# Strassen's seven products for three more chunks of a fused Fourier mixing and gated convolution kernel

## The chip, the cores and the metric

The kernel runs on one core of a Trainium2 chip. Its time is the device time of one launch in microseconds; it is given as the median of several runs. The profile is of one execution of the program on the chip, with the time of every instruction on each engine: PE (matrix products), PEld (the loading of a product's stationary operand, which runs beside PE), DVE (vector work), ACT (activations and copies), POOL (GpSimd) and SP (a queue that issues transfers). All values are 32-bit floating point. PE does a product of 32-bit values in two passes, so that one matmul of the program is two instructions of the profile.

## The reference

```
X = np.fft.fft(x, axis=1); X = np.fft.fft(X, axis=2); x = X.real     # x: 8 x 3136 x 256
h = np.maximum(x @ w_in, 0.0)                                        # w_in: 256 x 1024
conv_out = conv_w[0]*h[s-1] + conv_w[1]*h[s] + conv_w[2]*h[s+1]      # along the sequence
gate = 1 / (1 + exp(-conv_out))
return (h * gate) @ w_out                                            # w_out: 1024 x 256
```

## The kernel before

**Stages of a batch.** There are 8 batches b = 0 to 7 (the text calls b = 3 the fourth). The real Fourier transform along the sequence uses its symmetries: x of a batch is *folded* on DVE (sums and differences of rows and columns, `fold_ops`, 16 pieces per batch, L155 to L193 and L228), then eight *units* (`units`) multiply the folded x by tables of sines and cosines on PE (tiles `pd<-tab,w`) and put the results together on DVE (`fin`, L369 to L431, *unit sums*) into two tiles `pt` and `qt`. A unit has a PSUM bank `pd`, of which there is one; so a unit's first matmul waits until the DVE has read the sums of the unit before it.

**Chunks and steps.** A batch's outputs are made in 4 chunks c of rows; chunks 0, 1 and 2 have six tiles of 128 rows, chunk 3 six and a rest. Each chunk goes over 8 blocks f of 128 hidden features. A *step* is one (b, c, f): 32 steps per batch, 256 in all, numbered 32b + 8c + f. For a step, PE makes two products with `pt` and `qt` (`pb`, `pa`), ACT copies `pb` (L841), DVE combines the two to h with the ReLU (L849, twice), ACT makes the first tap (L855), a transfer of POOL's queue adds the middle one (L859), DVE the last (L864); ACT takes the sigmoid (L883), DVE the gate's product (L891), and then PE multiplies the gated rows by a block of w_out into `po` banks (`mm2`, L94), summed over the chunk's eight f. There are four `po` banks, given out in turn; each holds two row tiles of 256 columns. After f = 7 ACT copies the banks out (L1000) and SP writes them.

**What sets the order.** One loop over t writes every engine's queue by hand. In its round t stand: the sigmoid of step t-4, the products of step t+1 and their copies, the combine of t, the first tap of t, the last tap of t-3, the gate of t-4, the transfer of t, and the second product (`mm2`) of step t-5 (`LAG` is 5). Everything else (folds, units, loads, weights) is put beside it by `at(cycle, where, fn)`: in round `cycle`, at one of the places "first", "act", "dve", "late", "pool", "load" and "pe" of the round. `ends[b]` is the round by which the folds of batch b end and its units begin; the folds spread from `ends[b-1]` to `ends[b]`, one per round at most, and `free` finds a round not yet in `taken`; the units spread from `ends[b]` to the round 32b - 3. "late" (unit sums) is behind the gate on DVE, "dve" (folds, w_out's sums) between the combine and the last tap, "pe" behind `mm2`.

**Strassen's products.** `seven(s)` says for which chunks row tiles 4 and 5 are multiplied by Strassen's method in Winograd's form: for two f at a time, the 2 by 2 blocks of rows and features (`a11` to `a22`, 128 x 128 each) take seven matmuls of 128 columns in place of four of 256. Before, these are the chunks of the last two batches, but for the very last. In an odd f (round t with step t-5 odd), DVE makes four sums of the gated rows (`sums`, L933 to L936, tile `sv`); three of the seven products stand in `mm7` of that round, and the other four, which read `sv`, at the head of `mm2` of the next (`rest`). Differences of w_out's blocks (`forms`, L920, tile `TW`, four pieces) are made once. At the chunk's end the two banks `x` and `y` of the seven products are put together by one ACT copy (L967) and four DVE additions (`end`, L971 to L974), which stand behind everything of DVE's next round, since `rest` comes first. Such a chunk takes four `po` banks: two for row tiles 0 to 3, and `x` and `y`.

Of the kernel before, what the change touches and what calls it, by code (L numbers as in the profile page):

```python
# [37 lines left out]
def kernel(  # L38
# [11 lines left out]
    B, S, D = x.shape  # L50
# [11 lines left out]
    NF = F // P  # L62
# [30 lines left out]
    def mm(o, l, r, start, stop):  # L93
        nc.tensor.matmul(o, l, r, start=start, stop=stop, skip_group_check=True)  # L94
# [13 lines left out]
    def load_ops(b, h, eng, other=None, held=False):  # L108


        def plain():
            t = xp.tile([P, 8, 2, D], F32, name="xh", tag="xh")
            xh[b, h] = t
            if held:

                nc.gpsimd.memset(t[0:1, 0, 0, 0:1], 0.0)
            eng.dma_start(out=t[0:NP, 0:4], in_=bass.AP(
                tensor=x.tensor, offset=x.offset + (b * S + 1 + 2 * h) * D,
                ap=[[HQ * D, NP], [Q4 * D, 4], [1, 2 * D]]))

        def zero():
            t = xh[b, h]
            for s0, n, r in ((0, 4, 0), (4, 3, 1), (7, 1, 0)):
                (other or eng).dma_start(out=t[NP:KR, s0:s0 + n], in_=bass.AP(
                    tensor=x.tensor, offset=x.offset + (b * S + r * Q4) * D,
                    ap=[[D, 1], [Q4 * D, n], [0, 2], [1, D]]))

        def mirrored(m):
            def f():
                nc.gpsimd.indirect_dma_start(  # L130
                    out=xh[b, h][0:NP, 7 - m].rearrange("p q d -> p (q d)"),
                    out_offset=None,
                    in_=bass.AP(tensor=x.tensor, offset=x.offset,
                                ap=[[2 * D, B * S // 2], [1, 2 * D]]),
                    in_offset=bass.IndirectOffsetOnAxis(ap=idx[0:NP, 0:1], axis=0),
                    element_offset=(b * S + (4 - m) * Q4 - HO + 2 * (1 - h)) * D)
            return f
        return [plain] + [zero] * h + [mirrored(m) for m in range(4)]
# [451 lines left out]
    def spread(b, cs):  # L590

        for c in cs:
            ch = chunks[c]
            eb[b, c] = ebp.tile([P, HN], F32, name="eb", tag="eb")[:, 0:ch.k1 - ch.k0]
            nc.sync.dma_start(out=eb[b, c], in_=ed[b:b + 1, ch.k0:ch.k1].to_broadcast([P, ch.k1 - ch.k0]))
# [31 lines left out]
    chunks = [Chunk(c) for c in range(len(CUTS))]  # L627
# [132 lines left out]
    begin, us, row, flip, store, odd_first, even_first = units(0)  # L760
# [141 lines left out]
            nc.scalar.copy(out=left[:, f, b % 2 * LEFT:(b % 2 + 1) * LEFT], in_=gs[s][:, r])  # L902

    TW = {}
    due, ends_of = [], []

    def seven(s):

        b, c, f = s
        return b >= B - 2 and not (chunks[c].last and b % 2)  # L910

    def forms(i):

        one, two = wout[:, 0:NF:2], wout[:, 1:NF:2]
        b11, b12, b21, b22 = one[:, :, 0:P], one[:, :, P:D], two[:, :, 0:P], two[:, :, P:D]
        if i == 0:
            t = erp.tile([P, 4, NF // 2, P], F32, name="tw", tag="er")
            TW.update({k: t[:, j] for j, k in enumerate((5, 7, 6, 4))})
        k, x, y = ((5, b12, b11), (7, b12, b22), (6, b11, TW[7]), (4, b21, TW[6]))[i]
        vt(TW[k], x, y, op=ALU.subtract)  # L920

# [21 lines left out]
    def mm7(s):  # L943
# [9 lines left out]
        mm(x[:, 1], a12, wout[:, f, 0:P], False, last)  # L953
        mm(y[:, 0], a22, TW[4][:, m], m == 0, last)

        def rest():
            t = sums_of.pop(s)
            mm(y[:, 1], t[:, 0], TW[5][:, m], False, last)
            mm(y[:, 2], t[:, 1], TW[7][:, m], False, last)
            mm(x[:, 2], t[:, 2], TW[6][:, m], False, last)  # L960
# [17 lines left out]
    def mm2(s):  # L978
# [10 lines left out]
        if seven(s):  # L989
            tiles = tiles[:4]  # L990
# [15 lines left out]
        if not seven(s):  # L1006
            gs.pop(s)
        elif f % 2:
            mm7(s)
            gs.pop(s)  # L1010
            gs.pop((b, c, f - 1))
# [14 lines left out]
    ops, _, pres = fold_ops(0)  # L1026
# [43 lines left out]
    n = chunks[0].k1  # L1070
# [16 lines left out]
    per = len(chunks) * NF  # L1087
    LAG = 5
# [3 lines left out]
    taken = set()  # L1092

    def at(cycle, where, fn):
        side.setdefault((cycle, where), []).append(fn)
# [20 lines left out]


    ends = [9, 25, per + 13, 2 * per + 6][0:B] + [per * (b - 1) - 3 + max(11 - 4 * (b - 2), 0) for b in range(4, B)]
    def free(cycle):

        while cycle in taken:
            cycle += 1
        taken.add(cycle)
        return cycle

    for i in range(4):
        at(per * (B - 2) + i, "dve", lambda i=i: forms(i))
    feat = Feature()
    at(5, "load", feat.place)
    at(8, "dve", feat.signs)  # L1130
# [10 lines left out]
    for b in range(1, B):  # L1141
        begin, us, *_ = units(b)
        us = us[0:2] + us[5:7] + us[2:4] + us[7:] if b == 1 else us[0:4] + us[5:]

        c0 = ends[b] - 3 * (b == 1)
        n = per * b - (2 if b == 1 else 3) - c0
        at(max(c0, per * (b - 1) + 1), "pe", begin)
        cs = [c0 + i * n // len(us) for i in range(len(us) + 1)]
        if b > 1:
            cs[1:] = [c + (-1 if i == len(us) else 1) * (c % NF == LAG % NF) for i, c in enumerate(cs[1:], 1)]  # L1150
        for i, u in enumerate(us):
            k = cs[i + 1] - cs[i]
            j0 = int(b == B - 1)
            for j in range(j0, k):
                at(cs[i] + j, "pe", lambda u=u, j=j - j0, k=k - j0: u.matmuls(j, k))
            at(cs[i + 1], "act", u.copy)
            at(cs[i + 1], "late" if b > 1 else "dve", u.fin)
            if b > 1:
                taken.add(cs[i + 1])
        at(cs[-1] - 2, "load", lambda b=b: spread(b, range(len(chunks) - 2)))  # L1160
        at(per * b + 1, "load", lambda b=b: spread(b, [len(chunks) - 2]))
        at(per * b + NF, "load", lambda b=b: spread(b, [len(chunks) - 1]))
    for b in range(1, B):
        ops, singles, pres = fold_ops(b)
        c0, n = ends[b - 1], ends[b] - ends[b - 1]
        if b == 1:

            cs = [9, 11, 12, 13, 14, 16, *range(16, 26)]
            assert len(cs) == len(ops) and cs[-1] <= ends[1] and not taken & set(cs)
        else:  # L1170
            if b == 2:
                c0, n = c0 + 3, n - 3
            cs = [free(c0 + j * n // len(ops)) for j in range(len(ops))]
            assert cs[-1] < ends[b]
        if b + 1 < B:
            for h in range(2):
                for j, fn in enumerate(load_ops(b + 1, h, nc.sync)):
                    at(cs[len(ops) // 2 * (h + 1) - 1] + 1 + j, "load", fn)
        for j, fn in enumerate(ops):
            at(cs[j], "dve", fn)  # L1180
        for j, fn in singles.items():
            at(cs[j], "pool", fn)
        for j, fn in pres.items():
            at(cs[j], "act", fn)
# [3 lines left out]
    n = len(steps)  # L1188
# [6 lines left out]
    for t in range(n + LAG):  # L1195
# [20 lines left out]
        if t >= LAG and seven(steps[t - LAG]) and steps[t - LAG][2] % 2:  # L1216
            run_later = sums(steps[t - LAG])
        else:
            run_later = None
# [82 lines left out]
```

## Time and profile before

| | |
|---|---|
| median of 3 runs | 1147.53 us (1147.52 to 1147.59) |
| the profiled execution | 1147.18 us, its span 1145.4 us |
| busy on PE, DVE, ACT, POOL | 1127.9, 997.5, 892.1, 387.3 us |
| granted clock of PE | 1.0 |

The span is from the first to the last instruction, and what the time has beyond it (1.8 us) lies around it. A matmul's duration in the profile reaches until its results have drained, and the next one starts before that; so a row of n passes is best read by the distance from its start to the start of the next row. In a timeline a row is: start, length, engine, line, operation, out<-in, tile, count, and in brackets the idle time before it and who ended it.

### The profile page before, as it was taken

To read this page: it belongs to the slowest core of one execution; us is meant where nothing else is said; L and a number is where in the kernel's file an instruction comes from. 1 tells how busy PE (TensorE), PEld (TensorE's weight loads), DVE (VectorE), ACT (ScalarE), POOL (GpSimd) and SP (SyncE) were. 2 spreads that over 40 slices of the span, in tenths; PEclk is the share of its full clock that TensorE was granted. 3 is DMA by queue.
4 is the path that set the end of the run, shared out by engine and by line. 5 is a ranking of instruction groups with operands and counts; after the bars stand their busy time and mean duration, and the time that the engine had idled before them with its cause. 6 is when DMAs were issued, how large, how long until landed. Compare 5 with 4: busy or idle time off the path is not lost.

```text
span 1145.4 us, 15566 instructions
## 1 busy us (share of the span) xinstructions
PE 1127.9 (98%) x4992; PEld 889.4 (78%) x4992; DVE 997.5 (87%) x1596; ACT 892.1 (78%) x1700; POOL 387.3 (34%) x486
## 2 busy tenths in 40 slices
PE   6999999999999999999999999999999999999998
PEld 4777877788777877877777777777777888778777
DVE  8999899988888989888878888888887888898885
ACT  3788778877787778787878877887876878888884
POOL 5426523543345252424233232422222222222223
PEclk9999999999999999999999999999999999999999
DMA  8787985876767686757676766766655656666663
GB/s 238 193 131 160 171 169 113 189 168 137 169 129 162 127 194 142 175 117 158 136 174 135 152 136 125 180 139 124 135 118 101 137 119 139 139 142 130 129 123 95
DMA packets 107678, 167.53 MB, mean 146 GB/s; under 512 B 32174, under 2 KB 62920, under 8 KB 107597
## 3 DMA queue, kind: packets, MB, share of 16 engines
q0 software_dynamic: 42240, 115.87, 53.0%
q1 hardware_dynamic: 64616, 50.53, 15.7%
q8 instruction: 40, 0.66, 0.2%
q14 instruction: 41, 0.34, 0.1%
q10 hardware_dynamic: 741, 0.14, 0.1%
HBM read 37.80 MB, written 25.74 MB: 55 GB/s over the span
## 4 chain that ended last, share of the span: by engine, by line
PE 92%; DVE 5%; ACT 1%; issue 1%; POOL 0%; DVEq 0%; ACTq 0%
PE po L94 57%; PE pa L94 14%; PE pb L94 14%; PE pd L94 6%; DVE g L864 1%; DVE h L849 1%; DVE g L891 1%; DVE xh L166 0%; DVE xh L155 0%; DVE wout L662 0%; ACT nb L841 0%; ACT os L1000 0%; ACT g L883 0%; ACT pa L820 0%; DVE w L193 0%
## 5 line engine op out<-in xcount | busy, mean ns | idle before, releaser
L94 PE MATMUL po<-wout,g 128*128 128x256 f32 (+1 forms) x2960 | 669.2, 375 | 1.2 <-DVE g L891 1.1
L94 PEld LDWEIGHTS po<-wout,g 128*128 128x128 f32 x2960 | 553.8, 190 | 129.8 <-issue 16.9
L859 POOL DMA_DIRECT2D g<-h x256 | 219.7, 858 | 710.3 <-ACT g L855 406.5
L841 ACT ACTIVATE nb<-pb 128x386 f32<-128x386 f32 (+3 forms) x512 | 228.3, 501 | 194.5 <-PE pb L94 193.7
L849 DVE CUSTOM_DVE_ANT_0 h<-pa,nb 128x386 f32<-128x386 f32 (+3 forms) x512 | 265.5, 560 | 33.1 <-PE pa L94 14.3
L891 DVE TENSOR_TENSOR g<-g,h 128x770 f32<-128x770 f32 (+1 forms) x248 | 240.9, 971 | 48.6 <-ACT g L883 47.5
L864 DVE SCALAR_TENSOR_TENSOR g<-h,cw,g 128x770 f32<-128x770 f32 (+1 forms) x256 | 265.3, 1036 | 1.5 <-DMA g<-h 1.4
L883 ACT ACTIVATE g<-g,cw 128x770 f32<-128x770 f32 (+3 forms) x264 | 246.8, 938 | 16.3 <-DVE g L864 16.2
L855 ACT ACTIVATE g<-h,cw 128x770 f32<-128x770 f32 (+1 forms) x256 | 244.5, 955 | 0.0
L94 PE MATMUL pb<-qt,G 127*128 127x387 f32 (+2 forms) x512 | 213.5, 498 | 1.5 <-ACT nb L841 1.1
L94 PE MATMUL pa<-pt,G 128*128 128x387 f32 (+2 forms) x512 | 212.2, 495 | 1.0 <-ACT pa L820 0.7
L820 ACT ACTIVATE pa<-eb,ge 128x387 f32<-128x387 f32 (+2 forms) x256 | 155.6, 608 | 1.0 <-DVE h L849 0.4
L94 PEld LDWEIGHTS pa<-pt,G 128*128 128x128 f32 x512 | 96.6, 189 | 75.6 <-issue 19.0
L130 POOL DMA_INDIRECT xh<-in_x_dram,idx x64 | 100.3, 1567 | 19.3 <-issue 10.1
L94 PEld LDWEIGHTS pb<-qt,G 127*128 127x128 f32 x512 | 90.4, 190 | 8.3 <-ACT nb L841 2.7
L94 PE MATMUL pd<-tab,w 98*128 98x197 f32 (+2 forms) x448 | 94.5, 318 | 0.0
L94 PEld LDWEIGHTS pd<-tab,w 98*128 98x128 f32 (+1 forms) x448 | 79.5, 191 | 7.5
L1000 ACT COPY os<-po 128x256 f32<-128x256 f32 x182 | 53.5, 394 | 7.7 <-PE po L94 7.7
L177 POOL COPY w<-xh 98x4 f32<-98x4 f32 (+1 forms) x30 | 45.7, 1523 | 6.7 <-DVE xh L171 6.7
L155 DVE TENSOR_TENSOR xh<-xh 98x1020 f32<-98x1020 f32 (+1 forms) x32 | 38.7, 1213 | 0.7 <-DMA xh<-in_x_dram,idx 0.5
L166 DVE TENSOR_TENSOR xh<-xh 98x1024 f32<-98x1024 f32 (+1 forms) x32 | 38.9, 1216 | 0.1
L94 PEld LDWEIGHTS po<-tw,sv 128*128 128x128 f32 x168 | 23.0, 190 | 8.1 <-issue 2.5
(167 smaller groups left out, 538.0 us busy)
## 6 DMA issues: line engine op xcount, KB each, us to landing
g<-h POOLq DMA_DIRECT2D x192, 385.0 KB, 4.1
g<-h POOLq DMA_DIRECT2D x64, 416.0 KB, 4.3
out_dram<-os SPq DMA_DIRECT2D x96, 256.0 KB
xh<-in_x_dram SPq DMA_DIRECT2D x16, 784.0 KB
eb<-ed SPq DMA_DIRECT2D x16, 193.5 KB
raw<-in_moe_w_in_dram SPq DMA_DIRECT2D x4, 512.0 KB
raw<-in_moe_w_out_dram SPq DMA_DIRECT2D x1, 2048.0 KB
eb<-ed SPq DMA_DIRECT2D x8, 209.0 KB
```

The source lines that it names most:

```text
L94: nc.tensor.matmul(o, l, r, start=start, stop=stop, skip_group_check=True)
L130: nc.gpsimd.indirect_dma_start(out=xh[b, h][0:NP, 7 - m].rearrange("p q d -> p (q d)"), out_offset=None, in_=bass.AP(tensor=x.tensor, offs ...
L177: nc.gpsimd.tensor_copy(w[k, 0:2, qs, 0], t()[k, s:s + 2, :, 0])
L820: act(pa[s][:, 0:n], eb[b, c], AF.Copy, scale=ge[:, f:f + 1])
L841: act(nb[s][:, i, cols], p[:, cols], AF.Copy, scale=-1.0 if i else 1.0)
L849: nc.vector._custom_dve(TENSOR_ADD_SAT, out=to, in0=a[:, cols], in1=c[:, i, cols], s0=BIG, s1=0.0)
L855: act(gs[s], hs[s][:, 0:n], AF.Copy, scale=cw[:, 0, s[2]:s[2] + 1])
L859: nc.gpsimd.dma_start(out=gs[s], in_=hs[s][:, 1:1 + n], accum_op=ALU.add)
L864: stt(out=g, in0=h[:, k:k + n], scalar=cw[:, k, f:f + 1], in1=g, op0=ALU.mult, op1=ALU.add)
L883: act(gs[s][:, c], gs[s][:, c], AF.Sigmoid, scale=cw[:, 1, s[2]:s[2] + 1])
L891: vt(g, g, h[:, 0:r.stop], op=ALU.mult)
L1000: nc.scalar.copy(out=osb[:, j % 2], in_=pt[:, j % 2])
```

## The change

Chunk 1 of batches 3, 4 and 5 joins those multiplied by the seven products (`EXTRA`). The four pieces of w_out's differences move from rounds 192 to 195 to rounds 77, 95, 99 and 103. The rounds of a chunk of `EXTRA` in which DVE makes the four sums or the end (the five per chunk in `summing`: 110, 112, 114, 116 and 117 for batch 3) are closed to folds and to unit sums, which move to other rounds. `ends` of batches 5, 6 and 7 goes from 125, 157 and 189 to 128, 164 and 197, so that these folds end later and the units have 29, 25 and 24 rounds in place of 32; the last round of the units stays. The amount of fold and unit work is the same.

```
+    EXTRA = ((3, 1), (4, 1), (5, 1))
     def seven(s):
         b, c, f = s
-        return b >= B - 2 and not (chunks[c].last and b % 2)
+        return b >= B - 2 and not (chunks[c].last and b % 2) or (b, c) in EXTRA
...
+    ends[B - 3:] = [e + d for e, d in zip(ends[B - 3:], (3, 7, 8))]
...
-    for i in range(4):
-        at(per * (B - 2) + i, "dve", lambda i=i: forms(i))
+    for i, c in enumerate((77, 95, 99, 103)):
+        at(c, "dve", lambda i=i: forms(i))
+    summing = {per * b + NF * c + LAG + i for b, c in EXTRA for i in (1, 3, 5, 7, 8)}
+    taken.update(summing)
...
-            cs[1:] = [c + (-1 if i == len(us) else 1) * (c % NF == LAG % NF) for i, c in enumerate(cs[1:], 1)]
+            for i in range(1, len(cs)):
+                cs[i] += (-1 if i == len(us) else 1) * (cs[i] % NF == LAG % NF)
+                while cs[i] in summing:
+                    cs[i] += -1 if i == len(us) else 1
...
-            cs = [free(c0 + j * n // len(ops)) for j in range(len(ops))]
+            cs = [c for c in range(c0, c0 + n) if c not in taken]
+            if b > 4:
+                cs = [cs[j * len(cs) // len(ops)] for j in range(len(ops))]
+                taken.update(cs)
+            else:
+                cs = [free(c0 + j * n // len(ops)) for j in range(len(ops))]
```

On DVE, in rounds 110 and 111 (chunk 1 of batch 3 is in its second product there), stood before:

```order
L849 ISA h<-pa,nb 128x386 x2
L864 SCALAR_TENSOR_TENSOR g<-h,cw,g 128x770
L891 TENSOR_TENSOR g<-g,h 128x770
L381 TENSOR_TENSOR qt<-as,pd 128x393
L383 TENSOR_TENSOR qt<-pd,as 128x392
L849 ISA h<-pa,nb 128x386 x2
L155 TENSOR_TENSOR xh<-xh 99x4x255
L864 SCALAR_TENSOR_TENSOR g<-h,cw,g 128x770
L891 TENSOR_TENSOR g<-g,h 128x770
```

and in the same rounds now (its lines are one higher than the profile's behind the new line):

```order
L849 ISA h<-pa,nb 128x386 x2
L934 TENSOR_TENSOR sv<-g 128x128
L935 TENSOR_TENSOR sv<-g 128x128
L936 TENSOR_TENSOR sv<-sv,g 128x128
L864 SCALAR_TENSOR_TENSOR g<-h,cw,g 128x770
L937 TENSOR_TENSOR sv<-g,sv 128x128
L891 TENSOR_TENSOR g<-g,h 128x770
L849 ISA h<-pa,nb 128x386 x2
L864 SCALAR_TENSOR_TENSOR g<-h,cw,g 128x770
L891 TENSOR_TENSOR g<-g,h 128x770
L381 TENSOR_TENSOR qt<-as,pd 128x393
L383 TENSOR_TENSOR qt<-pd,as 128x392
```

The unit sums moved from round 110 to 111, the fold from 111 out of the pair (to 108), and the four sums stand alone in round 110.

On DVE at the end of that chunk, rounds 117 and 118, before:

```order
L849 ISA h<-pa,nb 128x386 x2
L166 TENSOR_TENSOR xh<-xh 99x1024
L864 SCALAR_TENSOR_TENSOR g<-h,cw,g 128x770
L891 TENSOR_TENSOR g<-g,h 128x770
L849 ISA h<-pa,nb 128x386 x2
L864 SCALAR_TENSOR_TENSOR g<-h,cw,g 128x770
L891 TENSOR_TENSOR g<-g,h 128x770
L427 TENSOR_TENSOR as<-pd,as 128x196
L428 TENSOR_TENSOR as<-pd,as 128x196
```

and now:

```order
L849 ISA h<-pa,nb 128x386 x2
L864 SCALAR_TENSOR_TENSOR g<-h,cw,g 128x770
L891 TENSOR_TENSOR g<-g,h 128x770
L972 TENSOR_TENSOR os<-os,po 128x256
L973 TENSOR_TENSOR os<-os,po 128x256
L974 TENSOR_TENSOR os<-os,po 128x128
L975 TENSOR_TENSOR os<-os,po 128x256
L849 ISA h<-pa,nb 128x386 x2
L864 SCALAR_TENSOR_TENSOR g<-h,cw,g 128x770
L891 TENSOR_TENSOR g<-g,h 128x770
L427 TENSOR_TENSOR as<-pd,as 128x196
L428 TENSOR_TENSOR as<-pd,as 128x196
```

The fold piece left round 117, the chunk's end came in behind the gate, and the unit sums of round 118 stayed where they were.

On PE at the same place (the products of steps 117 and 118, and behind each the second product and a unit's matmuls), before:

```order
L94 MATMUL pb<-qt,G 128x387
L94 MATMUL pa<-pt,G 128x387
L94 MATMUL po<-wout,g 128x256 x6
L94 MATMUL pd<-tab_112,w 128x197
L94 MATMUL pb<-qt,G 128x387
L94 MATMUL pa<-pt,G 128x387
L94 MATMUL po<-wout,g 128x256 x6
L94 MATMUL pd<-tab_112,w 128x197
```

and now:

```order
L94 MATMUL pb<-qt,G 128x387
L94 MATMUL pa<-pt,G 128x387
L94 MATMUL po<-wout,g 128x256 x4
L94 MATMUL po<-wout,g 128x128 x2
L94 MATMUL po<-tw,g 128x128
L94 MATMUL pd<-tab_112,w 128x197
L94 MATMUL pb<-qt,G 128x387
L94 MATMUL pa<-pt,G 128x387
L94 MATMUL po<-tw,sv 128x128 x3
L94 MATMUL po<-wout,sv 128x128
L94 MATMUL po<-wout,g 128x256 x6
L94 MATMUL pd<-tab_112,w 128x197 x2
```

The last pair of the chunk is split into three products in one round and four in the next, in front of the six ordinary ones with which chunk 2 begins; and a unit matmul more stands in the second round.

More of the change, by code (lines that the diff above doesn't have):

```diff
@@ L1149 @@
         if b > 1:
-            cs[1:] = [c + (-1 if i == len(us) else 1) * (c % NF == LAG % NF) for i, c in enumerate(cs[1:], 1)]
+            for i in range(1, len(cs)):
+                cs[i] += (-1 if i == len(us) else 1) * (cs[i] % NF == LAG % NF)
+                while cs[i] in summing:
+                    cs[i] += -1 if i == len(us) else 1
+            for i in range(len(us) - 1, 0, -1):
+                while cs[i] >= cs[i + 1] or cs[i] in summing:
+                    cs[i] -= 1
         for i, u in enumerate(us):
```

## The prediction

> **What bounds the kernel.** I began with the page: busy times, then the chain that ended last.
>
> ```profile
> span 1145.4 us, 15566 instructions
> PE 1127.9 (98%) x4992; PEld 889.4 (78%) x4992; DVE 997.5 (87%) x1596; ACT 892.1 (78%) x1700; POOL 387.3 (34%) x486
> PE 92%; DVE 5%; ACT 1%; issue 1%; POOL 0%; DVEq 0%; ACTq 0%
> ```
>
> PE is the bound: 98% of the span, 92% of the chain. A busy PE need not be full, so I next took the groups of PE instructions of 200 to 1110 us with the idle time before them (last column):
>
> ```profile
> L94 PE MATMUL po<-wout,g 128*128 128x256 f32 x2363 | 545.0, 379 | 0.0
> L94 PE MATMUL po<-tw,sv 128*128 128x128 f32 x162 | 22.4, 274 | 0.0
> ```
>
> PE waits for nobody there, with Strassen's products or without. So the change gains what its passes save on PE, and loses what new waits of PE cost; shorter work elsewhere gains nothing.
>
> **What the passes save.** The 379 and 274 ns above reach until the results are out, so they are not the price. The price is the distance between starts. First an ordinary round of chunk 0 to 2 without a unit, then two rounds with Strassen's products (timeline of PE):
>
> ```profile
> 803.07 0.81 PE L94 MATMUL pb<-qt,G 127*128 127x387 f32 x2
> 804.37 2.75 PE L94 MATMUL po<-wout,g 128*128 128x256 f32 x12
> 806.96 0.49 PE L94 MATMUL pb<-qt,G 127*128 127x387 f32 x1
> ...
> 1036.19 0.82 PE L94 MATMUL pb<-qt,G 127*128 127x387 f32 x2
> 1037.50 0.83 PE L94 MATMUL po<-tw,sv 128*128 128x128 f32 x6
> 1038.16 0.39 PE L94 MATMUL po<-wout,sv 128*128 128x128 f32 x2
> 1038.39 1.89 PE L94 MATMUL po<-wout,g 128*128 128x256 f32 x8
> 1040.12 0.82 PE L94 MATMUL pb<-qt,G 127*128 127x387 f32 x2
> 1041.42 2.33 PE L94 MATMUL po<-wout,g 128*128 128x256 f32 x12
> 1043.59 0.39 PE L94 MATMUL po<-tw,g 128*128 128x128 f32 x2
> 1043.82 0.49 PE L94 MATMUL pb<-qt,G 127*128 127x387 f32 x1
> ```
>
> A pass of 256 columns takes (806.96 - 804.37) / 12 = 0.2158 us. Of a pair's 14 short passes, eight read `sv`: 1038.39 - 1037.50 = 0.89. The x12 row at 1041.42 holds 8 long passes and 4 short ones, so the four take 2.17 - 8 x 0.2158 = 0.44, and the last two 0.23. Fourteen take 1.56 us; the eight long ones that they replace take 1.73. A pair saves 0.17. The whole rounds say the same within rounding: two ordinary ones 2 x 3.89 = 7.78, the pair 1043.82 - 1036.19 = 7.63, so 0.15. Three chunks have four pairs each: 12 x 0.15 = 1.8 to 12 x 0.17 = 2.0 us. I take 1.95. Unit matmuls only change rounds on PE: nothing.
>
> The Trainium skill (TensorE: Matmul & The Clock Gate, section on loading the stationary operand and on the back-to-back gap) says that a weight load takes its columns over 1.2 GHz, about 107 ns for 128, and that in a real stream the spacing is set by load and matmul together. If loads did not overlap here, my estimate by that page is 14 x 0.107 against 8 x 0.107, 0.64 more per pair against the 0.17 saved, +5.6 us in all. The trace disagrees on the overlap: eight short passes in 0.89 us, 111 ns each, leave no room for it.
>
> **What DVE gets in these rounds.** Durations of the added and the moved work (instructions on `sv`; groups of DVE, 500 to 860 us; w_out's differences):
>
> ```profile
> L936 DVE TENSOR_TENSOR sv<-g,sv x28: 281/285/1225, 896.0 to 1109.6; 128x128 f32<-128x128 f32 x28
> ...
> L166 DVE TENSOR_TENSOR xh<-xh 99x1024 f32<-99x1024 f32 x6 | 7.3, 1216 | 0.0
> L155 DVE TENSOR_TENSOR xh<-xh 99x1020 f32<-99x1020 f32 x6 | 7.3, 1210 | 0.0
> L192 DVE TENSOR_TENSOR w<-xh 99x508 f32<-99x508 f32 x6 | 4.1, 678 | 0.0
> ...
> L920 DVE TENSOR_TENSOR tw<-wout x2: 680/680/681, 865.9 to 870.6; 128x512 f32<-128x512 f32 x2
> ```
>
> And the load of DVE in the eight rounds 110 to 117 before, beside eight of batch 6 that have the seven products already (columns: PE, PEld, DVE, ACT, POOL busy):
>
> ```profile
> 511.26:545.16 33.90, 33.90 (x145) 27.02 (x145) 29.24 (x43) 26.06 (x48) 13.96 (x15) 1.00 0.74 164
> 918.00:952.00 34.00, 34.00 (x173) 27.85 (x172) 29.27 (x58) 26.38 (x47) 7.31 (x9) 1.00 0.58 116
> ```
>
> Rounds 110 to 117 lose two pieces of L155, one of the two of L166 and the pair L192 and L193: 1.21 + 1.21 + 1.22 + 1.36 = 5.0 us. They get 16 sums of 0.285 (4.6) and the end of the chunk, 1.57 (rows below). DVE has 29.24 - 5.0 + 6.1 = 30.3 us of work in 33.9 - 4 x 0.17 = 33.2: 91%, no worse than the 29.27 of 34.0 that batch 6 runs with an unstalled PE. The moved folds land in rounds without such work, at most one a round. Nothing of it reaches PE, since DVE's lag is covered: the four sums of round 110 are read by PE in round 111, behind the products that stand there. If that cover were gone, a late sum would cost PE as much as it is late. The pieces of w_out's differences (0.68 each) come between two folds or unit sums, and the next round takes them up. The loads of x move with the folds, by some rounds on SP and POOL's queue; the halves of batches 6 and 7 are still asked for ten rounds and more (3.9 us or longer each) before they are folded, so I cost them at nothing. On ACT a chunk has one narrow copy in place of two of its six.
>
> One rule of the skill bears on this (SBUF — State Buffer, who interferes with whom): a DVE instruction with two inputs in SBUF and a GpSimd one that reads SBUF block each other. The maximum of 1225 ns on L936 beside its median of 285 agrees in kind: one of 28 was held up. POOL's copies of folded columns could so make single sums 0.9 us later, which the cover of a round takes.
>
> **The chunk's end: two PSUM places.** This is where PE could newly wait. Chunk 2 begins in round 117 and takes three `po` banks at once; its third is the bank `x` of the seven products, which only DVE's third end addition frees. In batches 6 and 7 the next chunk takes `x` a round or more later, but for once. Round 205 of batch 6 has the same products, copies and widths:
>
> ```profile
> 922.14 1.19 ACT L1000 COPY os<-po 128x256 f32<-128x256 f32 x4
> 923.24 0.81 PE L94 MATMUL pb<-qt,G 127*128 127x387 f32 x2
> 923.34 0.99 ACT L883 ACTIVATE g<-g,cw 128x770 f32<-128x770 f32 x1
> 924.36 0.96 DVE L891 TENSOR_TENSOR g<-g,h 128x770 f32<-128x770 f32 x1 [1.61 <-ACT g L883]
> 925.21 0.39 PE L94 MATMUL po<-wout,sv 128*128 128x128 f32 x2
> 925.44 1.89 PE L94 MATMUL po<-wout,g 128*128 128x256 f32 x8
> 925.64 0.42 DVE L971 TENSOR_TENSOR os<-os,po 128x256 f32<-128x256 f32 x1 [0.31 <-PE po L94]
> 926.55 0.29 DVE L973 TENSOR_TENSOR os<-os,po 128x128 f32<-128x128 f32 x1
> 927.17 0.52 PE L94 MATMUL pd<-tab,w 98*128 98x196 f32 x2
> 927.21 1.02 DVE L849 CUSTOM_DVE_ANT_0 h<-pa,nb 128x386 f32<-128x386 f32 x2
> ```
>
> The third addition has read `x` at 926.84, and DVE goes on with the next round at 927.21, so that the end costs it 1.57. The fifth tile's matmul would start after eight long passes, at 927.17. The slack is 0.33 us, though the gate before had waited 1.61 for ACT. The one place where the next chunk does take `x` at once, at 1115.40, bears it out:
>
> ```profile
> 1115.40 2.79 PE L94 MATMUL po<-wout,g 128*128 128x256 f32 x12
> 1118.02 0.59 PE L94 MATMUL po<-wout,left 128*128 128x256 f32 x2
> ```
>
> Twelve passes in 2.62, against 12 x 0.2158 = 2.59: a wait of 0.03. I take 0.0 to 0.1 for the three places together.
>
> The second place is the one bank `pd`. Round 118 has unit sums right behind the end; PE's next unit matmul needs their reads of `pd` (L427, L428) done. Before:
>
> ```profile
> 545.16 0.81 PE L94 MATMUL pb<-qt,G 127*128 127x387 f32 x2
> 547.40 1.02 DVE L849 CUSTOM_DVE_ANT_0 h<-pa,nb 128x386 f32<-128x386 f32 x2
> 550.23 0.96 DVE L891 TENSOR_TENSOR g<-g,h 128x770 f32<-128x770 f32 x1 [0.88 <-ACT g L883]
> 551.66 0.35 DVE L428 TENSOR_TENSOR as<-pd,as 128x196 f32<-128x196 f32 x1
> 553.30 0.36 PE L94 MATMUL pd<-tab,w 99*128 99x99 f32 x2
> ```
>
> DVE began that round 2.24 behind step 118's products (547.40 - 545.16), and the slack was 553.30 - 552.01 = 1.29. In round 206, behind an end, it began 927.21 - 923.24 = 3.97 behind them: 1.73 later. Yet DVE then no longer idles 0.88 before the gate, and PE has between the same two points eight short passes on `sv` (0.89) and a second unit matmul more: 1.29 - 1.73 + 0.88 + 0.89 = 1.33 us of slack without that matmul. Cost nothing; if the 0.88 and the 0.89 were missing, PE would wait 0.44 a place.
>
> **Sum.** -1.95 + 0.05 = -1.9 us on the profiled execution, 1147.18 to 1145.3. The median of the runs shown lies 0.35 above that execution, so 1147.53 - 1.9 = 1145.6. That is 0.17% less, inside the 0.2% (2.3 us) about what a measurement of this kernel can tell from no change.
>
> **Rivals.**
> *The end comes late and PE waits for `x`* (slower). For it: only 0.33 us of slack, three times, and DVE's gate hangs on ACT's copies there. Against: round 117 has no fold and no unit sums, ACT there has no scaling and no unit copy, as in round 205. Each microsecond beyond 0.33 costs one, three times. It decides (above 1149.8) from 1.95 + 2.3 = 4.25 us, 1.4 a place. A DVE that came to round 117 a whole fold and a unit's sums behind (1.2 + 1.1, less the slack of 0.33) would give 3 x 2.0 = 6.0: 1151.6.
> *Half a wait.* `x` or `pd` late by 0.3 to 0.6 each time: 1 to 1.9 us, and the gain is eaten: 1146.6 to 1147.5, within 0.2%.
> *Weight loads set the pace* (the change then does not do what it says). If a load's 0.178 us (889.4 over 4992 on the page) could not overlap, 14 x 0.178 against 8 x 0.2158 is +0.77 a pair: 1147.5 + 9.2 = 1156.7. Against: 28 pairs already run at 111 ns a pass. The skill's rule above is the same mechanism at another price.
> *More is saved than the passes* (faster by over 0.2%). It needs 0.4 us more. PE's idle column is 0.0, so only small stalls at the start of products are to be had.
>
> **How the numbers follow.** Forecast 76%, half a wait 7%, late end or other new wait of PE 9%, weight loads 1%, more saved 7%. So faster 0.07, same 0.83, slower 0.10. The range goes from 1145.2 (2.0 saved and 0.3 more) to 1147.4 (half a wait).
>
> **What would show it.** In the changed profile a pair of chunk 1 in batches 3 to 5 is 0.15 to 0.17 us shorter on PE, less its unit matmuls; the first twelve passes of chunk 2 in round 117 take 2.59 to 2.65; the first `pd` matmul after round 118's unit sums starts without idle time; DVE busy grows by 12 x 1.14 + 3 x 1.57 = 18 us, and the idle column of PE stays 0.0. I am wrong if PE waits for DVE's end or for `sv` in these rounds.

## The result and the profile after

The changed kernel takes 1145.88 us (median of 22 runs, 1145.03 to 1146.94) against 1147.57 for the kernel before in runs between them (also 22): a ratio of 0.9984, 95% interval 0.9978 to 0.999. That is 1.7 us less, where 1.9 was forecast, and within 0.2% of no change. The profiled execution took 1145.46 us against 1147.18. Its page, the same lines as of before:

```profile
span 1143.7 us, 15776 instructions
PE 1127.2 (99%) x5064; PEld 890.4 (78%) x5064; DVE 1011.2 (88%) x1656; ACT 889.9 (78%) x1697; POOL 397.7 (35%) x486
PE 94%; DVE 3%; ACT 1%; issue 1%; DMA 0%; POOL 0%; DVEq 0%; ACTq 0%
```

and the groups of PE instructions of 200 to 1108 us:

```profile
L94 PE MATMUL po<-wout,g 128*128 128x256 f32 x2268 | 524.5, 379 | 0.0
L94 PE MATMUL po<-tw,sv 128*128 128x128 f32 x234 | 32.3, 274 | 0.0
```

PE has 72 instructions more (14 passes in place of 8 in each of 12 pairs), and its idle column is still 0.0. DVE has 13.7 us more work.

The time before about 370 us differs between executions, although nothing changes there but for one w_out difference in e9: the products of step 77 began at 369.97 to 371.23 us in the twelve traces of this study. So I compare one stretch in all of them, from the products of step 77 to those of step 255, the last. It holds every other change. Before (columns: PE, PEld, DVE, ACT, POOL busy, PE's clock, DMA share, GB/s):

```profile
370.06:1118.45 748.39, 748.39 (x3354) 595.10 (x3353) 646.26 (x1051) 600.12 (x1112) 214.46 (x276) 1.00 0.66 139
```

and after:

```profile
370.28:1116.73 746.45, 746.45 (x3426) 595.64 (x3425) 659.52 (x1111) 598.04 (x1109) 223.47 (x276) 1.00 0.66 140
```

748.39 - 746.45 = 1.94 us, on 12 pairs 0.162 each; the sum had 1.95. The start of this execution was 0.22 later, which makes 1.72 of the profiled time.

**The pair.** The first pair of chunk 1 of batch 3 has three of its products in round 110 and four in round 111. PE in these two rounds, before:

```profile
515.51 0.81 PE L94 MATMUL pb<-qt,G 127*128 127x387 f32 x2
...
519.40 0.50 PE L94 MATMUL pd<-tab,w 98*128 98x196 f32 x2
519.73 0.81 PE L94 MATMUL pb<-qt,G 127*128 127x387 f32 x2
...
523.63 0.50 PE L94 MATMUL pd<-tab,w 98*128 98x196 f32 x2
```

and after:

```profile
514.51 0.82 PE L94 MATMUL pb<-qt,G 127*128 127x387 f32 x2
...
518.21 0.52 PE L94 MATMUL pd<-tab,w 98*128 98x196 f32 x2
518.57 0.81 PE L94 MATMUL pb<-qt,G 127*128 127x387 f32 x2
...
519.87 0.83 PE L94 MATMUL po<-tw,sv 128*128 128x128 f32 x6
...
520.76 1.89 PE L94 MATMUL po<-wout,g 128*128 128x256 f32 x8
522.49 0.50 PE L94 MATMUL pd<-tab,w 98*128 98x196 f32 x2
```

From the products to the unit's matmuls the two rounds took 3.89 + 3.90 = 7.79 us and take 3.70 + 3.92 = 7.62: 0.17 less. The eight short passes on `sv` are 520.76 - 519.87 = 0.89, as they were in batch 7.

**The chunk's end.** Rounds 117 and 118, on PE and DVE (timeline):

```profile
545.68 2.76 PE L94 MATMUL po<-wout,g 128*128 128x256 f32 x12
545.88 0.42 DVE L972 TENSOR_TENSOR os<-os,po 128x256 f32<-128x256 f32 x1 [0.26 <-PE po L94]
546.79 0.29 DVE L974 TENSOR_TENSOR os<-os,po 128x128 f32<-128x128 f32 x1
547.45 1.02 DVE L849 CUSTOM_DVE_ANT_0 h<-pa,nb 128x386 f32<-128x386 f32 x2
548.27 0.87 PE L94 MATMUL pd<-tab,w 98*128 98x197 f32 x4
550.96 0.37 DVE L427 TENSOR_TENSOR as<-pd,as 128x196 f32<-128x196 f32 x1 [0.69 <-ACT as L418]
551.24 0.35 DVE L428 TENSOR_TENSOR as<-pd,as 128x196 f32<-128x196 f32 x1
552.87 0.36 PE L94 MATMUL pd<-tab,w 99*128 99x99 f32 x2
```

The twelve passes with which chunk 2 begins take 548.27 - 545.68 = 2.59 us, so its fifth tile did not wait for bank `x`. The third addition was done at 547.08, and that tile stood at 545.68 + 8 x 0.2158 = 547.41: 0.33 later. DVE had 0.26 in hand ahead of the end, for it waited there for PE's last product of the chunk. Round 118's unit sums had read `pd` at 551.59, 1.28 ahead of PE's next unit matmul.

### The profile page after: what moved, and what is told of

Read it like the earlier page. It is cut to its first block, busy times and chain, and to the rows that moved or that the text cites. A ratio compares the mean times of both kernels' runs of the same rounds, so it can differ in the third digit from the quotient of the medians.

```text
span 1143.7 us, 15776 instructions
## 1 busy us (share of the span) xinstructions
PE 1127.2 (99%) x5064; PEld 890.4 (78%) x5064; DVE 1011.2 (88%) x1656; ACT 889.9 (78%) x1697; POOL 397.7 (35%) x486
## 4 chain that ended last, share of the span: by engine, by line
PE 94%; DVE 3%; ACT 1%; issue 1%; DMA 0%; POOL 0%; DVEq 0%; ACTq 0%
PE po L94 58%; PE pb L94 15%; PE pa L94 15%; PE pd L94 6%; DVE g L864 1%; DVE h L849 1%; DVE g L891 1%; DVE wout L662 0%; ACT nb L841 0%; ACT os L1001 0%; DMA raw<-in_moe_conv_w_dram 0%; ACT g L883 0%; ACT pa L820 0%; ACT g L855 0%; DVE raw L668 0%
## 5 line engine op out<-in xcount | busy, mean ns | idle before, releaser
L94 PE MATMUL po<-wout,g 128*128 128x256 f32 (+1 forms) x2912 | 653.9, 373 | 1.2 <-DVE g L891 1.1
L94 PEld LDWEIGHTS po<-wout,g 128*128 128x128 f32 x2912 | 542.0, 190 | 124.6 <-issue 16.4
L891 DVE TENSOR_TENSOR g<-g,h 128x770 f32<-128x770 f32 (+1 forms) x248 | 240.4, 969 | 39.9 <-ACT g L883 39.0
L820 ACT ACTIVATE pa<-eb,ge 128x387 f32<-128x387 f32 (+2 forms) x256 | 155.8, 609 | 0.6 <-ACT ft L586 0.3
L130 POOL DMA_INDIRECT xh<-in_x_dram,idx x64 | 106.2, 1659 | 19.1 <-issue 9.1
L94 PE MATMUL pd<-tab,w 98*128 98x197 f32 (+2 forms) x448 | 92.1, 317 | 0.0
L177 POOL COPY w<-xh 98x4 f32<-98x4 f32 (+1 forms) x30 | 49.9, 1662 | 6.8 <-DVE xh L171 6.7
L94 PEld LDWEIGHTS po<-tw,sv 128*128 128x128 f32 x240 | 32.9, 191 | 11.4 <-issue 2.1
L166 DVE TENSOR_TENSOR xh<-xh 98x1024 f32<-98x1024 f32 (+1 forms) x32 | 38.9, 1215 | 0.1
```

Source lines behind the costliest of these rows:

```text
L130: nc.gpsimd.indirect_dma_start(out=xh[b, h][0:NP, 7 - m].rearrange("p q d -> p (q d)"), out_offset=None, in_=bass.AP(tensor=x.tensor, offs ...
L177: nc.gpsimd.tensor_copy(w[k, 0:2, qs, 0], t()[k, s:s + 2, :, 0])
L820: act(pa[s][:, 0:n], eb[b, c], AF.Copy, scale=ge[:, f:f + 1])
L891: vt(g, g, h[:, 0:r.stop], op=ALU.mult)
```

## The experiments

All edits are made to the changed kernel. "Stretch" is the time from the products of step 77 to those of step 255 in the profile; the medians and ratios stand against runs of the kernel before on the same chip.

| kernel | pairs against before | stretch, us | median, us (runs) | ratio to before, 95% |
|---|---|---|---|---|
| before | 0 | 748.39 | 1147.57 (22) | |
| after | 12 | 746.45 | 1145.88 (22) | 0.9984 [0.9978, 0.999] |
| e1, moves only | 0 | 748.39 | 1147.74 (11) | 1.0001 [0.9992, 1.001] |
| e2, products only | 12 | 746.53 | 1145.82 (11) | 0.9984 [0.9975, 0.9993] |
| e4, late end | 12 | 750.41 | 1149.44 (10) | 1.0018 [1.0009, 1.0027] |
| e5, late between | 12 | 746.45 | 1145.75 (10) | 0.9984 [0.9975, 0.9994] |
| e3, no Strassen | -28 | 752.97 | 1152.28 (4) | 1.004 [1.0024, 1.0055] |
| e6, six chunks, room | 24 | 746.00 | 1144.87 (11) | 0.9978 [0.9969, 0.9987] |
| e7, six chunks, no room | 24 | 746.87 | 1145.53 (11) | 0.9982 [0.9973, 0.9991] |
| e9, nine chunks | 36 | 746.23 | 1145.53 (10) | 0.9981 [0.9972, 0.999] |
| e11, six chunks, less room | 24 | 744.43 | 1143.89 (5) | 0.9963 [0.995, 0.9977] |
| e12, six chunks, room at the end | 24 | 745.61 | 1145.12 (9) | 0.9975 [0.9965, 0.9985] |

One more sum helps to read the table. The distance from one start on PE to the next is nearly always the same for the same two neighbouring passes. Added up over the stretch, the starts that come over 0.06 us later than usual (the median of the twelve traces) make 0.00 us in before, after, e1, e3, e5 and e11, 0.08 in e2, 3.96 in e4, 1.53 in e6, 2.41 in e7, 3.73 in e9 and 1.08 in e12. These late starts and 0.163 us for each pair give every stretch of the table to within 0.05 us.

### Which half of the change earns it

The moves alone: folds, unit sums and w_out's differences stand as in the changed kernel, but chunk 1 of batches 3 to 5 keeps ordinary products.

```
-        return b >= B - 2 and not (chunks[c].last and b % 2) or (b, c) in EXTRA
+        return b >= B - 2 and not (chunks[c].last and b % 2)
```

> The order of the changed kernel, with folds, unit sums and w_out's differences moved as there, but without Strassen's products in the three chunks. My theory (the gain is the 48 matmuls' passes on PE and nothing else; moved work is hidden in both places): the whole gain is gone, 1147.5 us (1147.2 to 1147.8), ratio 1.000 to the kernel before, and PE's idle time as before. Rival (the new rounds of folds and units are themselves worth something, or cost something): a time at least 0.5 us from 1147.5, such as 1146.7.

The stretch is 748.39, the same to the hundredth as before, and the ratio's interval holds 1. The moved folds, unit sums, loads and w_out differences cost nothing and gain nothing by themselves.

The products alone: the three chunks, with folds and unit sums where they stood before.

```
-    ends[B - 3:] = [e + d for e, d in zip(ends[B - 3:], (3, 7, 8))]
...
-    summing = {per * b + NF * c + LAG + i for b, c in EXTRA for i in (1, 3, 5, 7, 8)}
+    summing = set()
...
-            cs = [c for c in range(c0, c0 + n) if c not in taken]
-            if b > 4:
-                cs = [cs[j * len(cs) // len(ops)] for j in range(len(ops))]
-                taken.update(cs)
-            else:
-                cs = [free(c0 + j * n // len(ops)) for j in range(len(ops))]
+            cs = [free(c0 + j * n // len(ops)) for j in range(len(ops))]
```

> Strassen's products in the three chunks, w_out's differences early, but folds and unit sums in the rounds of the kernel before: they stand in the rounds with the four sums and with the chunk's end. My theory (DVE's lag has cover; only the end in round 117 has a slack of 0.33 us): DVE comes to the end about 0.4 us later than PE's products would let it, PE waits 0.1 to 0.3 for bank x at three places: 1146.2 us (1145.9 to 1146.8). Rival (the room that the change makes is what it needs): rounds 110 to 117 have 35.3 us of DVE work in 33.2, PE waits over 1 us at each of the three ends: above 1148.5.

Measured 1145.82 us and a stretch of 746.53, 0.08 over that of the changed kernel. I had thought the room worth 0.3 us or more, and it is worth a tenth. Here a fold piece (L166, 1.21 us) stands in round 117 ahead of the end, and the third addition falls late in one place of three:

```profile
546.54 2.85 PE L94 MATMUL po<-wout,g 128*128 128x256 f32 x12
547.86 0.29 DVE L974 TENSOR_TENSOR os<-os,po 128x128 f32<-128x128 f32 x1
549.23 0.52 PE L94 MATMUL pd<-tab,w 98*128 98x197 f32 x2
```

L974 is done at 548.15, only 0.12 before the fifth tile would start (546.54 + 1.73 = 548.27); that tile starts at 548.29, 0.14 behind L974, and the twelve passes take 2.69 in place of 2.59. With three chunks the closed rounds buy next to nothing.

No Strassen's products anywhere, to price the pair over all of them:

```
-        return b >= B - 2 and not (chunks[c].last and b % 2) or (b, c) in EXTRA
+        return False
```

> The changed kernel's order with no chunk multiplied by the seven products at all: ten chunks (forty pairs) fewer than in the changed kernel, 28 pairs fewer than in the kernel before. My theory (0.1625 us of PE per pair, wherever it stands, and nothing else): 40 x 0.1625 = 6.5 us over the changed kernel, 1152.4 us (1151.9 to 1152.9). Rival (in batches 6 and 7, where DVE has no or few folds, the products were worth another amount than in batches 3 to 5): outside 1151.4 to 1153.4.

The stretch grows to 752.97: 4.58 us over before, which has 28 pairs (0.164 each), and 6.52 over after, which has 40 (0.163 each). On average a pair is worth the same in batches 6 and 7 as in batches 3 to 5, and none of it is lost in waits.

### What the end's 0.33 us is worth

Four more DVE instructions of 128 x 256 on an unused half of a scratch tile, in one place per chunk: right ahead of the end (rounds 117, 149, 181), or four rounds earlier.

```
+    def ballast():
+        for _ in range(4):
+            vt(left[:, 0:4, LEFT:P], left[:, 0:4, LEFT:P], left[:, 4:8, LEFT:P], op=ALU.max)
+
+    for b, c in EXTRA:
+        at(per * b + NF * c + LAG + 8, "late", ballast)     # e4; LAG + 4 in e5
```

> The changed kernel with four extra DVE operations of 128 x 256 (about 1.3 us together) behind the gate of rounds 117, 149 and 181, ahead of the chunk's end. My theory (the end's third addition frees bank x with 0.33 us to spare, and beyond that PE waits one to one): x comes about 1.0 us later, PE waits 0.7 to 0.9 at three places: 1148.2 us (1147.6 to 1148.8). Rival (x is not what PE would wait for, there is more cover): 1145.9, as the changed kernel.

> The changed kernel with the same four extra DVE operations behind the gate of rounds 113, 145 and 177, between two rounds with sums. My theory (DVE's lag there has several us of cover): 1145.9 us (1145.6 to 1146.3), as the changed kernel, with DVE up to 1.3 us more behind the products for a few rounds. Rival (DVE is full in these rounds, and added work comes through to PE): 1.3 us for each of three places, 1149.8; half of it 1147.8.

Ahead of the end, the chunk of batch 3 (timeline of DVE and PE):

```profile
545.94 1.79 DVE L1135 TENSOR_TENSOR left<-left 128x256 f32<-128x256 f32 x4
546.08 1.89 PE L94 MATMUL po<-wout,g 128*128 128x256 f32 x8
547.84 0.42 DVE L972 TENSOR_TENSOR os<-os,po 128x256 f32<-128x256 f32 x1
548.75 0.29 DVE L974 TENSOR_TENSOR os<-os,po 128x128 f32<-128x128 f32 x1
549.18 1.10 PE L94 MATMUL po<-wout,g 128*128 128x256 f32 x4 [1.21 <-DVE os L974]
```

The fifth tile would have started at 546.08 + 1.73 = 547.81 and starts at 549.18, 1.37 us late. My additions held DVE for 547.84 - 545.94 = 1.90 us. The 0.26 that DVE had in hand absorbs a part, the 0.33 of slack another; and from the end of L974 (549.04) to PE's start another 0.14 passes: 1.90 - 0.26 - 0.33 + 0.14 = 1.45 against 1.37 (DVE came to the additions 0.08 earlier than in the changed kernel, counted from PE's first pass). The two other tiles are 1.19 and 1.18 late. At all three the next pass starts another 0.07 late. All in all the stretch grows by 3.96 us, 1.32 a place, and the kernel is 0.18% slower than before. So the mechanism of the slower rival holds: at this one size of the addition, what DVE's end is late beyond the slack costs PE as much, three times. I had expected 1148.2 us; the additions were bigger than I thought (0.47 us each between starts), so it is 1149.44.

The same work four rounds earlier costs 0.00: stretch 746.45, and 1145.75 us. What DVE does between the ends is covered, as the prediction said, here four such instructions a place.

### How many chunks can have it

Chunks 1 and 2 of batches 3 to 5, with the five rounds of each closed by the changed kernel's own rule:

```
-    EXTRA = ((3, 1), (4, 1), (5, 1))
+    EXTRA = tuple((b, c) for b in (3, 4, 5) for c in (1, 2))
```

> Chunk 2 of batches 3, 4 and 5 as well, six chunks in place of three, with room made by the same rule (ten rounds a batch closed to folds and unit sums; some folds then stand two to a round). My theory: another 12 pairs, -1.95, and the rounds of sums are at most 91% full on DVE: 1143.9 us (1143.6 to 1144.6). Rival (the folds that are crowded into the other rounds make DVE late, and PE waits): above 1145.5.

Measured 1144.87 us, a microsecond more than I expected. Waits of PE, 380 to 1108 us:

```profile
PE pa L94 <- ACT pa L820: 0.5, 1, 0.5
PE pd L94 <- ACT g L883: 0.3, 1, 0.3
```

They are not at a chunk's end. By the gaps between PE's starts three places lose 0.5 us (473.20), 0.3 (515.56) and 0.7 (729.88). The last one:

```profile
724.90 3.32 POOL L177 COPY w<-xh 99x4 f32<-99x4 f32 x1
725.05 1.21 DVE L166 TENSOR_TENSOR xh<-xh 99x1024 f32<-99x1024 f32 x1
...
727.17 1.02 DVE L891 TENSOR_TENSOR g<-g,h 128x832 f32<-128x832 f32 x1
728.30 0.91 ACT L222 ACTIVATE rt<-w,turn 98x256 f32<-98x256 f32 x2 [1.86 <-POOL h L826]
729.25 0.58 ACT L820 ACTIVATE pa<-eb,ge 128x386 f32<-128x386 f32 x1
729.88 0.92 PE L94 MATMUL pa<-pt,G 128*128 128x386 f32 x2 [0.46 <-ACT pa L820]
```

POOL's copy of four columns, which belongs to the fold, lasts 3.32 us beside DVE's fold piece and gate; ACT's scaling (L222) waits for it (the profile names a POOL instruction behind the copy, L826, done 0.08 later), the seed of `pa` (L820) stands behind that on ACT, and PE waits for the seed. The wait at 515.56 has the same chain, behind a copy of 2.41 us at 511.64. The one at 473.20 has another: DVE's combine at 469.03 had waited 1.09 us for POOL (L826), which stood behind the issue of a load of x (L130, 4.13 us); with a piece of w_out's differences behind it as well, DVE had read `pd` for the unit sums (L401) only at 473.05, and PE's unit matmul started 0.15 after that. With ten rounds per batch closed, fold pieces stand closer together; that this crowding is why POOL's lateness reaches PE here and not elsewhere is argued from the order, and e11 below agrees with it.

The six chunks without any room, that is with the edits of e2 as well:

> The same six chunks, but folds and unit sums in the rounds of the kernel before, among the sums. My theory: DVE has 70.8 us of work in the 66.4 of rounds 110 to 125, but starts the end of round 125 only about 0.7 us late, so PE waits about 0.5 at three places and 0.1 at the three of round 117: 1145.7 us (1144.6 to 1146.6), so that with six chunks the room is worth 1 to 2 us, where with three it was worth nothing. Rival (room never matters): 1143.9.

Measured 1145.53 us, and 1145.7 was expected; but the places were only in part those that I had named. Two of the five at which PE waits (timeline of DVE and PE):

```profile
552.77 0.35 DVE L428 TENSOR_TENSOR as<-pd,as 128x196 f32<-128x196 f32 x1
553.27 0.44 PE L94 MATMUL pd<-tab,w 99*128 99x99 f32 x2 [0.34 <-DVE as L428]
...
581.45 1.89 PE L94 MATMUL po<-wout,g 128*128 128x256 f32 x8
583.21 0.29 DVE L974 TENSOR_TENSOR os<-os,po 128x128 f32<-128x128 f32 x1
583.64 0.67 PE L94 MATMUL po<-wout,g 128*128 128x256 f32 x2 [0.30 <-DVE os L974]
```

Both banks that the prediction named now hold PE up: `x` at the end of chunk 2 (583.64 against 581.45 + 1.73 = 583.18, 0.46 late), and `pd` behind the end of chunk 1, where round 118 has the sums of chunk 2's first pair as well. In both, PE starts 0.14 to 0.15 after DVE's read is done (583.50, 553.12). I had counted waits for the ends alone, 0.5 at all three of chunk 2 and 0.1 at those of chunk 1. PE waits at two ends of chunk 2 (1.1 us together) and at none of chunk 1; the rest, 1.3 us at three places, is for `pd`, which I had not counted. That the total came close is luck.

Less room, in two runs: of the six chunks' five rounds only the first and the last two are closed, or only the last two.

```
-    summing = {per * b + NF * c + LAG + i for b, c in EXTRA for i in (1, 3, 5, 7, 8)}
+    summing = {per * b + NF * c + LAG + i for b, c in EXTRA for i in (1, 7, 8)}     # e11; (7, 8) in e12
```

> Six chunks (1 and 2 of batches 3 to 5), with only three of a chunk's five rounds closed: the first sums, the last sums and the end. Folds stand one to a round again, some with sums, and none right behind the piece whose copies POOL makes; no unit sums with four additions stand with sums behind an end. My theory: what six chunks lost with all rounds closed (1.5 us) came from folds crowded into other rounds, not from too little room; from the ledger DVE's lag stays at 4.1 or less and comes to the ends at 2.5 or less. So all 24 pairs count: -3.9 to the kernel before, with 0.1 to 0.3 of waits: 1143.9 us (1143.5 to 1144.4). Rival (DVE is simply too full with six chunks): 1144.8 or more, as with all rounds closed.

> The same with two rounds a chunk closed, the last sums and the end, so that rounds 118, 150 and 182 hold sums and a unit's four additions behind an end, as with no room at all. My theory (there the one bank pd comes late to the next unit; with no room PE waited 0.5, 0.3 and 0.3 there, and 0.5 twice for x at chunk 2's end, where a fold stood in the end's round): the waits for pd stay, 0.9 to 1.2 us, those for x go: 1144.8 us (1144.4 to 1145.3). Rival (the waits came from DVE's load in general): as with no room, 1145.5 or more.

e11 takes 1143.89 us, 0.9963 of before (0.995 to 0.9977): better than both kernels. The group of PE on `sv`, 380 to 1108 us:

```profile
L94 PE MATMUL po<-tw,sv 128*128 128x128 f32 x306 | 42.3, 274 | 0.0
```

24 pairs, 748.39 - 744.43 = 3.96 us, 0.165 each: all of it, with no wait left. Against e7 the room and the moves are worth 746.87 - 744.43 = 2.44 us in the stretch. In e12, where the first round of each chunk is open again, the waits for `x` are gone, but PE again waits for `pd`, 0.30 us each at 552.83 and 690.89 and 0.33 at 703.99: 1145.12 us, in the range. The first two stand where I expected them, in rounds 118 and 150, behind an end. Round 182 has none; the third is in round 153, one round after DVE had the fold's pair (L192, L193) and the sums together. So with the last two rounds closed nothing waits for `x`, closing the first one as well removes the waits for `pd`, mostly where a chunk with sums follows an end, and the two rounds between (`i` = 3 and 5) bring nothing here: closing them too is all that sets e6, with its waits, apart from e11.

Chunks 0, 1 and 2 of batches 3 to 5, with no closed round (w_out's differences in rounds 69, 77, 95 and 99, so that they are there in time):

```
-    EXTRA = ((3, 1), (4, 1), (5, 1))
+    EXTRA = tuple((b, c) for b in (3, 4, 5) for c in (0, 1, 2))
...
-    for i, c in enumerate((77, 95, 99, 103)):
+    for i, c in enumerate((69, 77, 95, 99)):
...
-    summing = {per * b + NF * c + LAG + i for b, c in EXTRA for i in (1, 3, 5, 7, 8)}
+    summing = set()
```

> Chunks 0, 1 and 2 of batches 3, 4 and 5: nine chunks, no room made, w_out's differences a little earlier. On PE alone 36 pairs save 5.85: 1141.7. My theory (the change can be had on PE only while DVE has time): DVE has about 123.4 + 2 x 6.1 = 135.7 us of work in a batch of 134.4, besides its waits for ACT, so it becomes the bound in these batches and gives back 2 to 5 us in each: 1148 to 1157. Rival (DVE's cover is enough): 1141.7 to 1143.

I expected DVE to become the bound and 1148 us or more; it is 1145.53. 36 pairs at 0.163 are 5.87 us, of which 3.7 are lost again. The waits that the profile names are now for unit sums:

```profile
PE pd L94 <- DVE qt L383: 1.1, 2, 0.6
PE pd L94 <- DVE as L371: 0.8, 1, 0.8
```

By the gaps between PE's starts six waits for `pd` in batches 3 to 5 make 3.5 us of it, and late starts of the rest's products (`left`) at 860.91 the other 0.2. In batches 3 to 5 DVE is busy for 387.47 of 408.78 us, 95%, and still is not the bound. My sum of its load was too high in two terms: it took batch 3's 123.4 us for every batch, where the changed kernel has 120.6 on average, and it priced two more chunks at 12.2 us, where they add 129.16 - 120.59 = 8.6, for the reason that the next section gives.

## Why the prediction came out right

**What the passes save**: -1.95 forecast, -1.94 measured in the stretch, and 0.163 a pair when all 40 are taken out. The distance between starts was the right price; that it came out to a hundredth is more than a reading of 1.8 to 2.0 could promise. In the changed kernel 40 pairs and in e11 52 run at 111 ns a pass, so the loads are covered by the passes. The Trainium skill's price of a weight load (TensorE: Matmul & The Clock Gate, section on loading the stationary operand), 128 columns over 1.2 GHz, gave the prediction's estimate of +5.6 us for loads that do not overlap; the runs show that they do.

**The bank `x`**: slack 0.33 read from batch 6, 0.33 in the changed kernel; 0.0 of the 0.0 to 0.1 that I took. What I did not know is that the bank passes on 0.14 us after DVE's read: only 0.19 of the slack could be used. The slower rival was real in kind, as e4 shows, but nothing in round 117 makes the end late.

**DVE's load in rounds 110 to 117**: 30.3 of 33.2 us forecast, 1.1 more than before. The prediction counted between PE's products, but DVE is behind them, and in the changed kernel it makes the chunk's end only after those of step 118 (543.49). So here are DVE's own rounds, from its combine of step 110 to that of step 118, before and after:

```profile
513.50:547.40 33.90, 33.90 (x146) 27.02 (x145) 29.91 (x44) 26.06 (x48) 14.53 (x14) 1.00 0.74 164
513.37:547.45 34.08, 34.08 (x174) 27.92 (x173) 29.82 (x58) 27.50 (x49) 14.86 (x13) 1.00 0.75 167
```

DVE has 29.82 us there, 87%, and 0.1 less than before. e1, with the moves alone, has 25.67 (513.53 to 547.43). So the pieces that moved out took 4.2 us with them, not 5.0, and the sums and the end bring 4.2, not 6.1: both terms were too big.

**The bank `pd`**: 1.28 left, where 1.33 was worked out without the second unit matmul. DVE's start behind the products, 547.45 - 543.49 = 3.96 (3.97 forecast), held. With that matmul's 0.36 the sum would be 1.69. What took the rest is ACT's copy (L418), which I had not counted: ahead of the unit sums DVE idles 0.69 for it, where before it idled 0.19:

```profile
551.38 0.37 DVE L427 TENSOR_TENSOR as<-pd,as 128x196 f32<-128x196 f32 x1 [0.19 <-ACT as L418]
```

That is 0.50 less; 0.09 more came from the gate, which starts 1.86 behind the combine in place of 2.83, 0.97 earlier where 0.88 was taken. The hit is partly luck, for the two omissions nearly cancel.

**The mis-sized term** is DVE's growth: 18 us forecast, 13.7 on the page (997.5 to 1011.2). Round 110 of the changed kernel shows why:

```profile
514.30 0.28 DVE L934 TENSOR_TENSOR sv<-g 128x128 f32<-128x128 f32 x1
514.50 0.28 DVE L935 TENSOR_TENSOR sv<-g 128x128 f32<-128x128 f32 x1
514.71 0.28 DVE L936 TENSOR_TENSOR sv<-sv,g 128x128 f32<-128x128 f32 x1
514.91 1.01 DVE L864 SCALAR_TENSOR_TENSOR g<-h,cw,g 128x770 f32<-128x770 f32 x1
515.84 0.28 DVE L937 TENSOR_TENSOR sv<-g,sv 128x128 f32<-128x128 f32 x1
516.04 0.95 DVE L891 TENSOR_TENSOR g<-g,h 128x770 f32<-128x770 f32 x1
```

A sum is 0.28 us long, but the next instruction starts after 0.20: four cost 0.81, not 1.14, and 12 x 0.81 + 3 x 1.57 = 14.4. I read PE by starts and the sums by durations. That changed nothing for the forecast, as DVE is not the bound, but it misled me about e9.

**The moves** were costed at nothing, loads included; e1 measures 0.00. What the prediction did not say is that the room they make is of next to no use to three chunks (0.08 us, e2), and worth 2.4 us with six if three of the five rounds are closed (e11 against e7).

**The other rivals.** Half a wait at `x` or `pd` did not occur in the changed kernel and did with six chunks and no room (e7). Loads that set the pace, and more saved than the passes, are both out by 0.162 a pair.

## What to carry to other kernels

On an engine that never waits, price an edit by the distance between starts, and do so for the engine that feeds it as well; durations of short instructions overlap and overstate both. A release of a PSUM bank is a deadline: find the moment at which the other engine wants it, and spend the slack between the two knowingly: in these runs late work cost nothing up to it and its full length beyond. When room is made for new work, find which of the reserved places carries a deadline (in these runs the last two rounds of a chunk, and the first where chunks follow each other) and leave the others open.

## What was new about the hardware

POOL's copies of four columns (L177) in the trace of e6 (count, shortest, median and longest in ns, first and last start in us):

```profile
L177 POOL COPY w<-xh x30: 500/1816/3340, 19.1 to 886.2; 98x4 f32<-98x4 f32 x15, 99x4 f32<-99x4 f32 x15
```

The same small copy takes 0.50 to 3.34 us. The one at 724.90 ended at 728.22, as DVE's run of instructions with two inputs in SBUF did (L891, 728.19). So it is with all 22 copies of 0.7 us and more: each ends 0.03 to 0.05 us behind such an instruction of DVE. The other eight, of 0.50 to 0.54 us, met such instructions for 0.1 us at most. The Trainium skill (SBUF — State Buffer, who interferes with whom) says that GpSimd's port is shared with DVE's second one, as an exclusive lock; these rows agree, and give the price, up to 2.8 us for a copy. The prediction had only thought of DVE being held up. The one long sum that it shows (L936, 1.23 us, at 1109.56 in the kernel before) stood beside POOL's own gate product of the last steps (L894, 1109.35 to 1110.63), not beside such a copy.

From the end of DVE's read of a PSUM bank to the start of the matmul that waits for it, 0.14 us passed at `x` (549.04 to 549.18, 583.50 to 583.64) and 0.15 at `pd` (553.12 to 553.27). The pass behind one that waited so starts late as well: 0.29 us after it at the three tiles of e4 and the two of e7, where 0.216 is usual.

The twelve kernels are the same program up to step 77 (e9 but for one DVE instruction), and yet their executions, one of each, reach it up to 1.3 us apart (369.97 to 371.23), as much as most of the effects studied here. Why, no run shows. The stretch behind it is free of that: where an edit costs nothing it comes out the same to the hundredth, 748.39 in before and e1, 746.45 in after and e5.
